# Moving one batch's key sums beside a projection in chunk 1 of a linear attention and GELU feed-forward kernel

## The chip, the cores and the metric

The kernel runs on one core of a Trainium2 chip. The metric is the device time of the whole program in microseconds, the median of several executions. TensorE is called PE below, VectorE DVE, ScalarE ACT, GpSimd POOL and SyncE SP, as in the profile.

## The reference

Linear attention without softmax, an RMS norm per head, and a two-layer feed-forward block with the exact GELU, all in float32:

```python
kv = np.einsum('bhsd,bhse->bhde', k, v)            # 8 batches, 8 heads, 576 tokens, 64 wide
out = np.einsum('bhsd,bhde->bhse', q, kv)
rms = np.sqrt(np.mean(out * out, axis=-1, keepdims=True) + 1e-06)
attn = out / rms * g_norm
x = attn.transpose(0, 2, 1, 3).reshape(4608, 512)
h = x @ w_in                                       # 512 x 2048
g = 0.5 * h * (1 + erf(h / sqrt(2)))
return g @ w_out                                   # 2048 x 512
```

## The kernel before

The 4608 tokens are nine chunks of 512. For each chunk the kernel makes the attention output of the next chunk beside the two layers of this one. The order on every engine is the order in which the code calls the instructions; nothing is reordered, and each engine works through its own queue.

Attention has four steps. `sum_kv` (L176) adds up k^T v of a batch with 80 small matmuls into one PSUM bank, and `place_kv` copies the bank into the SBUF tile `kv[b % 2]`: ACT one copy (L187), DVE two for the swapped halves (L189). `project` (L230) multiplies queries with these, half a chunk's heads at a time, 24 small matmuls into the two banks a0 and a1. `square` and `reduce` give sums of squares (ACT L262, L263, DVE L272), `swap` (ACT L283) and `rsqrt` (DVE, L292 to L314) the norm, and `scale` (DVE L327 and L323) applies it to one of four blocks. For chunks from 2 on, `add_blocks` (L358), `high_block` and `low_block` (L363, L368) then make seven combinations of the blocks, each split into a high and a low half in the fp32r format.

Chunks 0 and 1 do the feed-forward block plainly. A chunk is 16 slots, one per 128 columns of the hidden layer. In slot i, `layer1` does 12 matmuls of 128x512 into one of the two banks h0 and h1 (L662), `gelu` reads it twice (ACT L671, L672), `rest` makes the low half gl of the result (DVE L677), and `second_layer` of the slot before does 12 matmuls (L685), of which every third takes gl. Chunks from 2 on use products of combined 256-wide blocks (seven in place of eight), for which chunk 1 must combine the weights: `sum_weights` adds the blocks of the first layer (DVE L423 and L434; ACT L449 the high half, DVE L455 the low one), as often per slot as `HALVES` says; `sum_out` adds those of the second on POOL (L542), in the slots of `SUMS`; `split_out` splits them (in the kernel before ACT L1018, DVE L1019). SP sends the results to DRAM (L412) and loads what comes next: keys and values in `load_kv` (L130 the main block, 512 KB, L152 the tail, 128 KB), queries (L211), and weights of chunk 2 into a ring (`fetch`, L506) or for good (`keep`, L535).

In chunk 1 (c = 1) the order of a slot is: layer 1 on PE; `spread_matmuls`, which holds projections of chunk 2 and the sums of batch 3; GELU; squares if the slot is in `SQUARES`; `sum_weights` with `rest`; the reduction; `sum_out` and `split_out`; `spread_work` (the norm and the sums of blocks); `second_layer` of the slot before; and `later`, which holds `swap`, the loads and the copies of `place_kv`. Tiles for all these pieces are taken from and given back to one list, `free`, first in, first out, so that a step which takes or gives back earlier changes which tile each later step gets.

Of the kernel before, what the change touches and what calls it, by code (L numbers as in the profile page):

```python
# [37 lines left out]
def linear_attn_rms_gelu_ffn(  # L38
# [19 lines left out]
    B, NP = kv_main.shape[:2]  # L58
# [16 lines left out]
    def bank(name):  # L75
        return psum.tile([P, 512], F32, name=name)

    turn = {"h": 0, "a": 0}

    def next_bank(kind):  # L80

        turn[kind] ^= 1
        return bank(f"{kind}{turn[kind]}")
# [35 lines left out]
    def load_kv(b, p):  # L119

        early = b == 0 or (b == 1 and p > 1)
        if early:
            main = late_tile(f"w_out{NF - 1 - p if b == 0 else NF - 3 - p}")
        elif b == 2 and p > 1:
            main = block_tile(f"s{p - 1}", F32)
        elif b > 2 and p > 1:
            names["keys", p], main = take(stays=True)
        else:
            main = work.tile([P, 2 * DM], I32, name="kv_main", bufs=2).bitcast(F32)
        nc.sync.dma_start(out=main, in_=kv_main[b, p])  # L130
        main = main.rearrange("p (a n) -> p a n", a=2)[:KROWS]
        if b == 0:
            tails = late_tile(f"w_in{NF - 1}")[:TAIL].rearrange("p (a n) -> p a n", a=NP)
            if p == 0:
                nc.sync.dma_start(out=tails, in_=kv_tail[0])
            tail = tails[:, p]
        else:
            at = slice((p - 2) * 2 * P, (p - 1) * 2 * P)
            if early:
                tail = late_tile(f"w_in{NF - 5}")[:, at]  # L140
            elif b == 2 and p > 1:
                if p == 2:
                    kv_ps["tails"] = block_tile("s0", F32)
                tail = kv_ps["tails"][:, at]
            elif b > 2 and p > 1:
                if p == 2:
                    names["keys", 0], kv_ps["tails"] = take(stays=True)
                tail = kv_ps["tails"][:, at]
            else:
                tail = work.tile([P, 2 * P], I32, name="kv_tail", bufs=2).bitcast(F32)  # L150
            tail = tail[:TAIL]
            nc.sync.dma_start(out=tail, in_=kv_tail[b, :, p])  # L152
        tail = tail.rearrange("p (a n) -> p a n", a=2)
        parts = [main[:, :, j * P:(j + 1) * P] for j in range(NJ)] + [tail]
        kv_in[b, p] = [(t[:, 0], t[:, 1]) for t in parts]

    def free_keys():
        free.extend(names.pop(("keys", n)) for n in (2, 3, 0))

    kv_ps = {}  # L160

    def rows(r):
        return slice(r * D, (r + 1) * D)

    def sum_kv(b, pairs, ps=None):

        first = 0
        if ps is None:
            first = pairs[0]
            ps = kv_ps[b, first] = next_bank("a")  # L170
        for p in pairs:
            n = p - first
            for j, (k, v) in enumerate(kv_in.pop((b, p))):

                for r in (slice(0, D), slice(D, 2 * D)):
                    nc.tensor.matmul(  # L176
                        out=ps[r, n * D:(n + 1) * D], lhsT=k[:, r], rhs=v[:, r],
                        start=(j == 0), stop=(j == NJ),
                    )

    def place_kv(b, pairs):

        ps = kv_ps.pop((b, pairs[0]))
        ps = ps[:, :len(pairs) * D].rearrange("p (n d) -> p n d", d=D)
        at = slice(pairs[0], pairs[-1] + 1)
        t = kv[b % 2]
        nc.scalar.copy(out=t[:, at, 0], in_=ps)  # L187
        for r in range(2):
            nc.vector.tensor_copy(out=t[rows(r), at, 1], in_=ps[rows(1 - r)])  # L189
# [196 lines left out]
    def piece(x):  # L386
        return x.rearrange("p (k a n) -> p k a n", k=2, a=2)
# [139 lines left out]
    def take(dtype=F32, stays=False, first=()):  # L527
        name = next(n for n in [*(n for n in first if n in free), *free]
                    if not (stays and n in RINGS))
        free.remove(name)  # L530
        return name, block_tile(name, dtype)[:, :2 * DM]

    def keep(key):
        t = resident[key] = block_tile(KEPT_IN[key[1]], F32R)[:, AWAY:AWAY + 2 * DM]
        nc.sync.dma_start(out=t.bitcast(F32), in_=products[key])  # L535
# [139 lines left out]
    def rest(gh, gl, h):  # L675

        nc.vector.tensor_tensor(out=gl, in0=h, in1=gh.bitcast(F32), op=ALU.subtract)  # L677
        return gh, gl
# [106 lines left out]
    for d in range(0, 2 * D, BLK):  # L785
        h = d // D * D
# [39 lines left out]
    ps = next_bank("a")  # L826
# [47 lines left out]
    for half in range(2):  # L874
# [6 lines left out]
        n = 2 + half  # L881
# [21 lines left out]
    g, h, acc, sums, names = {}, {}, {}, {}, {}  # L903

    def spread_work(c, i):


        nxt = attn[c + 1]
        if c == 0:
            if i in (3, 5, 7, 9):  # L910
                nxt.squares(BLOCKS[i // 2 - 1])
            if i == 11:
                nxt.inv = nxt.rsqrt()
            if 12 <= i < 15:
                for n in ((0,), (1, 2), (3,))[i - 12]:
                    nxt.scale(n)
            if i in (13, 14):
                nxt.split_x(i - 13)
            return
        if i == 7:  # L920
            nxt.inv = nxt.rsqrt()
        for n in {8: (0, 1), 9: (2, 3)}.get(i, ()):
            nxt.scale(n)
        if i == 11:
            names["spots"], t = zip(*(take(stays=True) for _ in range(2)))
            nxt.spots = {"T3": t[0][:, :DM], "T4": t[0][:, DM:], "T2": t[1][:, :DM]}
        for k in {11: ("T3", "T1"), 12: ("T2", "T4")}.get(i, ()):
            nxt.add_blocks(k)
        for n in {13: (0, 4, 5), 14: (1, 2), 15: (3, 6)}.get(i, ()):
            names[c + 1, n], t = take(F32R, True, (f"w_in{i - 1}",))  # L930
            nxt.high_block(n, piece(t))
            nxt.low_block(n, nc.vector)
        if i == 15:
            free.extend(names.pop("spots"))
            LATE.extend(free[-2:])

    def spread_matmuls(c, i):
        nxt = attn[c + 1]
        if i in ((1, 4) if c else (2, 6)):
            nxt.project(i // 4)  # L940
        if i == 10 and not c:
            nxt.swap()
        if i == (8 if c else 12):
            sum_kv(c + 2, range(NP))
            if c:
                free_keys()

    halves = [(j, second) for j in range(NF // 2) for second in range(2)]

# [19 lines left out]
    def raw_out(j):  # L969

        t = [parts["out", 2 * j + n].rearrange("p (a n) -> p a n", a=2) for n in range(2)]
        product_out(place_out(j, 0), t[0][:, :, :HALF])
        product_out(place_out(j, 4), t[1][:, :, :HALF])
        product_out(place_out(j, 3), t[1][:, :, HALF:])
# [51 lines left out]
    def send():  # L1026

        for x in sent:
            if isinstance(x, str):
                free.append(x)  # L1030
            else:
                product_out(*x)
        sent.clear()

    def later(c, i):

        if i in (8, 9):
            raw_out(i - 2)
        if i == 6:
            attn[c + 1].swap()  # L1040
        if i in (3, 4):
            load_kv(c + 2, i - 1)
        if i in (6, 7):
            attn[c + 2].load(i - 6)
        if i == 9:
            place_kv(c + 2, range(NP))
        if i in KEYS_AHEAD:
            load_kv(c + 3, KEYS_AHEAD.index(i))
        send()
        if f"w_in{i}" not in KEPT_OUT:  # L1050
            free.append(f"w_in{i}")
        if i == 4:
            free.append("w_out3")
        for n in {11: (0, 1), 12: (2, 3, 4), 13: (5,)}.get(i, ()):
            fetch(n)
        for n in {10: (0,), 11: (1,), 13: (2,), 15: (3,)}.get(i, ()):
            keep(RESIDENT[n])

    SUMS = {2: 1, 5: 2, 8: 3, 11: 4, 13: 5}
    SPLITS = {2: 0, 3: 1, 6: 2, 9: 3, 12: 4}  # L1060
    SQUARES = (1, 2, 4, 5)
    HALVES = {0: 2, 1: 1, 2: 1, 3: 2, 4: 1, 5: 1, 6: 1, 7: 1, 8: 1, 10: 2, 11: 1, 12: 1, 13: 1, 14: 0}
    KEYS_AHEAD = (9, 10, 12, 14)
    order = list(range(3, len(weights)))

    last = [2]
# [32 lines left out]
    for s in range(PLAIN * NF):  # L1099
        c, i = divmod(s, NF)  # L1100
# [43 lines left out]
        else:  # L1144
            spread_matmuls(c, i)
            g[s] = gelu(h.pop(s))
            nxt, k = attn[c + 1], SQUARES.index(i) if i in SQUARES else None
            if k is not None:
                sq = nxt.square(BLOCKS[k])
            sum_weights(i, HALVES.get(i, 0), lambda: g.update({s: rest(*g[s])}))  # L1150
            if k is not None:
# [180 lines left out]
    for c in range(FAST, NCH):  # L1332
# [4 lines left out]
        for j, second in parts_of_layer1():  # L1337
# [19 lines left out]
            if c == FAST:  # L1357
                if (j, second) in LAST_SPLITS:
                    n = NJ2 - 2 + LAST_SPLITS.index((j, second))
# [7 lines left out]
            if second and j in (1, 3, NJ2 - 1) or (j, second) == (NJ2 - 1, False):  # L1367
                n = j // 2 - (last and not second)
# [69 lines left out]
```

## Time and profile before

| | us |
|---|---|
| Median of three executions | 770.92 (770.61 to 771.04) |
| The profiled execution: its own time | 770.82 |
| Its span from the first to the last instruction | 769.0 |
| PE busy in it | 763.9 |
| DVE busy | 588.2 |
| ACT busy | 368.4 |
| POOL busy | 181.7 |

Chunk 1's slots lie between 113 and 206 us of the span. The chain that ended last goes back from the last instruction, at each step to what released it, and gives each engine its share. In the order of time a row is the start, the time from the start to the last end of the merged instructions, engine, line, operation, output and inputs, shape and count; a bracket gives idle time ahead of it and what ended that.

### The profile page before, as it was taken

To read this page: it belongs to the slowest core of one execution; us is meant where nothing else is said; L and a number is where in the kernel's file an instruction comes from. 1 tells how busy PE (TensorE), PEld (TensorE's weight loads), DVE (VectorE), ACT (ScalarE), POOL (GpSimd) and SP (SyncE) were. 2 spreads that over 40 slices of the span, in tenths; PEclk is the share of its full clock that TensorE was granted. 3 is DMA by queue.
4 is the path that set the end of the run, shared out by engine and by line. 5 is a ranking of instruction groups with operands and counts; after the bars stand their busy time and mean duration, and the time that the engine had idled before them with its cause. 6 is when DMAs were issued, how large, how long until landed. Compare 5 with 4: busy or idle time off the path is not lost.

```text
span 769.0 us, 16770 instructions
## 1 busy us (share of the span) xinstructions
PE 763.9 (99%) x6588; PEld 723.5 (94%) x6588; DVE 588.2 (76%) x1041; ACT 368.4 (48%) x720; POOL 181.7 (24%) x155
## 2 busy tenths in 40 slices
PE   8999999999999999999999999999999999999998
PEld 7888888888899999999999999999999999999998
DVE  3999867989968974889388947795789578965783
ACT  3777635533564543465244714463446343632460
POOL 1000025433737200630045002700270018001200
DMA  9999963869999998999899989988998999799974
GB/s 344 408 407 375 360 199 127 298 233 316 372 332 333 366 397 320 322 325 374 328 331 325 362 342 329 323 289 323 324 336 274 340 321 322 254 315 351 324 245 170
DMA packets 90178, 244.90 MB, mean 318 GB/s; under 512 B 8948, under 2 KB 31988, under 8 KB 90100
## 3 DMA queue, kind: packets, MB, share of 16 engines
q1 hardware_dynamic: 90096, 243.83, 88.5%
q8 instruction: 52, 0.85, 0.4%
q14 instruction: 26, 0.21, 0.1%
q10 hardware_dynamic: 4, 0.00, 0.0%
HBM read 207.09 MB, written 34.08 MB: 314 GB/s over the span
## 4 chain that ended last, share of the span: by engine, by line
PE 98%; DMA 1%; ACT 0%; DVE 0%; issue 0%
PE acc L1221 24%; PE acc L551 22%; PE h L551 13%; PE acc L685 11%; PE a L1221 11%; PE h L662 11%; DMA w_out<-kv_main 1%; PE a L230 1%; PE acc L176 1%; PE a L176 1%; PE h L652 1%; PE acc L230 1%; PE h L820 0%; PE acc L886 0%; PE h L774 0%; ACT gl L809 0%
## 5 line engine op out<-in xcount | busy, mean ns | idle before, releaser
L685 PE MATMUL acc<-w_out,gh 128*128 128x512 f32 x256 | 79.3, 391 | 0.0
L551 PE MATMUL acc<-w_in,w_in 128*128 128x256 f32 x600 | 78.9, 276 | 0.0
L551 PEld LDWEIGHTS acc<-w_in,w_in 128*128 128x128 f32 x600 | 73.0, 188 | 0.1
L662 PE MATMUL h<-x,w_in 128*128 128x512 f32 x264 | 70.3, 390 | 0.0
L662 PEld LDWEIGHTS h<-x,w_in 128*128 128x128 f32 x264 | 49.3, 188 | 10.8 <-issue 0.3
L685 PEld LDWEIGHTS acc<-w_out,gh 128*128 128x128 f32 x256 | 47.7, 188 | 10.2 <-issue 0.2
L685 PE MATMUL acc<-w_out,gl 128*128 128x512 f32 x128 | 49.8, 389 | 0.0
L551 PE MATMUL h<-w_in,w_in 128*128 128x256 f32 x360 | 48.1, 277 | 0.0
L1221 PE MATMUL acc<-w_in,w_in 128*128 128x256 f32 x378 | 47.9, 276 | 0.0
L542 DVE TENSOR_TENSOR gl<-acc,gh 128x256 f32<-128x256 f32 (+1 forms) x77 | 33.9, 441 | 17.4 <-ACT gh L564 13.3
L1221 PEld LDWEIGHTS acc<-w_in,w_in 128*128 128x128 f32 x378 | 45.1, 188 | 0.0
L671 ACT ACTIVATE gh<-h 128x512 fp32r<-128x512 f32 x32 | 19.1, 598 | 53.1 <-PE h L662 53.1
L1221 PE MATMUL acc<-w_in,w_out 128*128 128x256 f32 x354 | 44.4, 276 | 0.0
L551 PEld LDWEIGHTS h<-w_in,w_in 128*128 128x128 f32 x360 | 44.2, 188 | 0.1
L1221 PEld LDWEIGHTS acc<-w_in,w_out 128*128 128x128 f32 x354 | 42.1, 188 | 0.0
L1221 PE MATMUL acc<-w_in,x 128*128 128x256 f32 x324 | 40.8, 276 | 0.0
L1221 PEld LDWEIGHTS acc<-w_in,x 128*128 128x128 f32 x324 | 38.6, 188 | 0.0
L551 PE MATMUL acc<-x,w_in 128*128 128x256 f32 x270 | 37.1, 276 | 0.0
L1188 POOL TENSOR_TENSOR w_in<-x,w_in 128x512 f32<-128x512 f32 x5 | 7.4, 1474 | 113.7 <-ACT x L583 113.7
L551 PEld LDWEIGHTS acc<-x,w_in 128*128 128x128 f32 x270 | 33.6, 188 | 0.0
L262 ACT ACTIVATE sq<-acc 128x512 f32<-128x512 f32 x10 | 6.0, 602 | 57.2 <-PE acc L230 57.2
L272 DVE TRANSPOSE_TENSOR_REDUCE part<-sq 128x16 f32<-128x512 f32 x33 | 23.3, 706 | 12.6 <-ACT sq L262 12.6
(360 smaller groups left out, 1956.2 us busy)
## 6 DMA issues: line engine op xcount, KB each, us to landing
w_in<-products_in SPq DMA_DIRECT2D x168, 512.0 KB, 5.1
w_in<-products_out SPq DMA_DIRECT2D x133, 512.0 KB, 5.3
products_in<-w_in SPq DMA_DIRECT2D x38, 256.0 KB, 5.4
w_in<-w_in SPq DMA_DIRECT2D x16, 512.0 KB, 10.2
w_out<-w_out SPq DMA_DIRECT2D x16, 512.0 KB, 10.2
q<-qT SPq DMA_DIRECT2D x15, 512.0 KB, 6.9
kv_main<-kv_main SPq DMA_DIRECT2D x14, 512.0 KB, 6.4
w_out<-kv_main SPq DMA_DIRECT2D x8, 512.0 KB, 7.0
```

The costliest lines, as they stand in the source:

```text
L176: nc.tensor.matmul(out=ps[r, n * D:(n + 1) * D], lhsT=k[:, r], rhs=v[:, r], start=(j == 0), stop=(j == NJ),)
L230: nc.tensor.matmul(out=ps[rows(h), p % 2 * HALF + a:p % 2 * HALF + e], lhsT=kv[b % 2][rows(half), p, h ^ half], rhs=q[rows(half), h, a:e], ...
L262: nc.scalar.activation(out=sq, in_=ps, func=AF.Square)
L272: nc.vector.tensor_reduce(out=self.part[:, 2 * k[0] + k[1], :], in_=sq.rearrange("p (b d) -> p b d", d=BLK), op=ALU.add, axis=AX.X, apply_ ...
L542: return eng.tensor_tensor(out=out, in0=x, in1=y, op=op)
L551: nc.tensor.matmul(out=out, lhsT=y, rhs=x[:, z, kb], start=first and kb + i == 0, stop=kb == 1 and i == 2, skip_group_check=True,)
L652: nc.tensor.matmul(out=h[:, half * HALF:(half + 1) * HALF], lhsT=ws[i].bitcast(F32)[:, p * P:(p + 1) * P], rhs=at.block((p // 2, half))[:, ...
L662: nc.tensor.matmul(out=h, lhsT=parts["in", i][:, w][:, p * P:(p + 1) * P], rhs=at.x[p][:, x], start=(m + p == 0), stop=(m == 2 and p == NP ...
L671: nc.scalar.activation(out=gh, in_=h, func=AF.Gelu)
L685: nc.tensor.matmul(out=ps, lhsT=x[:, ts], rhs=parts["out", i][:, w], start=(i == 0 and m == 0), stop=(m == 2 and (i == NF - 1 or (i, t) == ...
L1188: eng.tensor_tensor(out=out, in0=x, in1=y, op=op)
L1221: nc.tensor.matmul(out=self.bank[name][a][:, a * HALF:(a + 1) * HALF], lhsT=x[:, at], rhs=y, start=(k in (0, 2, 1) and n + p + m == 0 and ...
```

## The change

In chunk 1 alone: the projection's second half (of chunk 2's attention) goes from slot 4 to slot 6, and batch 3's key sums from slot 8 to slot 6, right behind it. The sums go into the h bank that layer 1 doesn't use at that moment, in place of an a bank, and `place_kv` follows at once, ahead of slot 6's GELU, in place of at the end of slot 9. The squares of the second half go from slots 4 and 5 to 6 and 7, the swap from 6 to 7, the inverse root from 7 to 8, the scaling from slots 8 and 9 to 9 and 10. One weight sum goes from slot 10 to slot 5. Two loads of batch 4's keys come a slot earlier (12 to 11 and 14 to 13), and the tiles of batch 3's keys are given back two slots earlier.

```diff
--- before.py
+++ after.py
@@ -917,9 +917,9 @@
             if i in (13, 14):
                 nxt.split_x(i - 13)
             return
-        if i == 7:
+        if i == 8:
             nxt.inv = nxt.rsqrt()
-        for n in {8: (0, 1), 9: (2, 3)}.get(i, ()):
+        for n in {9: (0, 1), 10: (2, 3)}.get(i, ()):
             nxt.scale(n)
         if i == 11:
             names["spots"], t = zip(*(take(stays=True) for _ in range(2)))
@@ -936,14 +936,17 @@
 
     def spread_matmuls(c, i):
         nxt = attn[c + 1]
-        if i in ((1, 4) if c else (2, 6)):
-            nxt.project(i // 4)
+        if i in ((1, 6) if c else (2, 6)):
+            nxt.project(i // 6 if c else i // 4)
         if i == 10 and not c:
             nxt.swap()
-        if i == (8 if c else 12):
+        if i == 12 and not c:
             sum_kv(c + 2, range(NP))
-            if c:
-                free_keys()
+        if i == 6 and c:
+            ps = kv_ps[c + 2, 0] = bank(f"h{1 - turn['h']}")
+            sum_kv(c + 2, range(NP), ps)
+            free_keys()
+            place_kv(c + 2, range(NP))
 
     halves = [(j, second) for j in range(NF // 2) for second in range(2)]
 
@@ -1036,14 +1039,12 @@
 
         if i in (8, 9):
             raw_out(i - 2)
-        if i == 6:
+        if i == 7:
             attn[c + 1].swap()
         if i in (3, 4):
             load_kv(c + 2, i - 1)
         if i in (6, 7):
             attn[c + 2].load(i - 6)
-        if i == 9:
-            place_kv(c + 2, range(NP))
         if i in KEYS_AHEAD:
             load_kv(c + 3, KEYS_AHEAD.index(i))
         send()
@@ -1058,9 +1059,9 @@
 
     SUMS = {2: 1, 5: 2, 8: 3, 11: 4, 13: 5}
     SPLITS = {2: 0, 3: 1, 6: 2, 9: 3, 12: 4}
-    SQUARES = (1, 2, 4, 5)
-    HALVES = {0: 2, 1: 1, 2: 1, 3: 2, 4: 1, 5: 1, 6: 1, 7: 1, 8: 1, 10: 2, 11: 1, 12: 1, 13: 1, 14: 0}
-    KEYS_AHEAD = (9, 10, 12, 14)
+    SQUARES = (1, 2, 6, 7)
+    HALVES = {0: 2, 1: 1, 2: 1, 3: 2, 4: 1, 5: 2, 6: 1, 7: 1, 8: 1, 10: 1, 11: 1, 12: 1, 13: 1, 14: 0}
+    KEYS_AHEAD = (9, 10, 11, 13)
     order = list(range(3, len(weights)))
 
     last = [2]
```

PE around the projection's second half, in slot 4 before (h, a and acc are PSUM banks, kv the sums of two batches; L230 is the projection):

```order
L662 MATMUL h_1654<-s_1367,w_in_559 128x512
L230 MATMUL a_1667<-q,kv_69 64x128 x2
L230 MATMUL a_1668<-q,kv_68 64x256 x2
L230 MATMUL a_1667<-q,kv_68 64x128 x2
L230 MATMUL a_1667<-q,kv_69 64x128 x2
L230 MATMUL a_1668<-q,kv_68 64x256 x2
L230 MATMUL a_1667<-q,kv_68 64x128 x2
L685 MATMUL acc_1510<-w_out_567,gh 128x512 x2
```

The projection has wide matmuls ahead of it and behind it, and nothing of it is left in slot 4 now. PE around the key sums (L176), in slot 8 before:

```order
L662 MATMUL h_1883<-s_1367,w_in_737 128x512
L176 MATMUL a_1896<-kv_main 64x64 x8
L176 MATMUL a_1896<-kv_tail 64x64 x2
L176 MATMUL a_1896<-kv_main 64x64 x8
L176 MATMUL a_1896<-kv_tail 64x64 x2
L176 MATMUL a_1896<-x_1646 64x64 x8
L176 MATMUL a_1896<-s_1648 64x64 x2
L176 MATMUL a_1896<-x_1715 64x64 x8
L176 MATMUL a_1896<-s_1648 64x64 x2
L685 MATMUL acc_1510<-w_out_774,gh 128x512 x2
```

The sums too have wide matmuls on both sides, write an a bank, and are gone from slot 8 now. PE in slot 6 now, from the last three groups of the projection on:

```order
L230 MATMUL a_1771<-q,kv_69 64x128 x2
L230 MATMUL a_1772<-q,kv_68 64x256 x2
L230 MATMUL a_1771<-q,kv_68 64x128 x2
L176 MATMUL h_1785<-kv_main 64x64 x8
L176 MATMUL h_1785<-kv_tail 64x64 x2
L176 MATMUL h_1785<-kv_main 64x64 x8
L176 MATMUL h_1785<-kv_tail 64x64 x2
L176 MATMUL h_1785<-x_1646 64x64 x8
L176 MATMUL h_1785<-s_1648 64x64 x2
L176 MATMUL h_1785<-x_1697 64x64 x8
L176 MATMUL h_1785<-s_1648 64x64 x2
L685 MATMUL acc_1510<-w_out_679,gh 128x512 x2
```

The projection now goes straight over into the sums, and the sums' output is an h bank; what follows is slot 5's second layer.

DVE from the kv copies of slot 9 to slot 11's gl before (z and w are the staged weight sums, o the attention output, sq a spread norm):

```order
L189 COPY kv1_69<-a0_1896 64x4x64 x2
L434 TENSOR_TENSOR w_2065<-z_1943,z_1945 128x256
L434 TENSOR_TENSOR w_2065<-z_1943,w_1947 128x256
L677 TENSOR_TENSOR gl_2062<-h1_2048,gh_2061 128x512
L423 TENSOR_TENSOR z_2071<-w_in12_928 128x512
L423 TENSOR_TENSOR z_2073<-w_in13_999 128x512
L434 TENSOR_TENSOR w_2075<-z_2073 128x256
L434 TENSOR_TENSOR w_2075<-w_2075,z_2071 128x256
L455 TENSOR_TENSOR w_in2_2069<-w_2065,w_in2_2069 128x2x256
L434 TENSOR_TENSOR w_2118<-z_2071,z_2073 128x256
L434 TENSOR_TENSOR w_2118<-z_2071,w_2075 128x256
L677 TENSOR_TENSOR gl_2113<-h0_2099,gh_2112 128x512
```

The copies open the stretch, and all the rest of it are weight sums and two gl. The same stretch now, from the end of slot 9's work on:

```order
L423 TENSOR_TENSOR z_2067<-w_in12_928 128x512
L423 TENSOR_TENSOR z_2069<-w_in13_999 128x512
L434 TENSOR_TENSOR w_2071<-z_2069 128x256
L434 TENSOR_TENSOR w_2071<-w_2071,z_2067 128x256
L677 TENSOR_TENSOR gl_2064<-h1_2050,gh_2063 128x512
L327 STREAM_TRANSPOSE sq_2075<-y_1964 128x512
L323 TENSOR_TENSOR o_1492<-o_1492,sq_2075 128x512
L327 STREAM_TRANSPOSE sq_2078<-y_1964 128x512
L323 TENSOR_TENSOR o_1492<-o_1492,sq_2078 128x512
L434 TENSOR_TENSOR w_2118<-z_2067,z_2069 128x256
L434 TENSOR_TENSOR w_2118<-z_2067,w_2071 128x256
L677 TENSOR_TENSOR gl_2113<-h0_2099,gh_2112 128x512
```

The two kv copies and one weight sum's low half (L455) with its two adds (L434) have left this stretch, and two scale steps (L327 with L323) stand in it, ahead of slot 11's gl.

ACT from slot 6's GELU on before:

```order
L671 ACTIVATE gh_1781<-h1_1768 128x512
L672 ACTIVATE h1_1768<-h1_1768 128x512
L449 CAST x0_1785<-w_1740 128x2x256
L1018 CAST w_in3_1798<-w_in0_1749 128x2x256
L1018 CAST w_in2_1801<-w_in0_1749 128x2x256
L283 ACTIVATE t_1816<-part_1508 32x64 x4
L671 ACTIVATE gh_1844<-h0_1831 128x512
L672 ACTIVATE h0_1831<-h0_1831 128x512
L449 CAST w_out3_1848<-w_1791 128x2x256
```

No kv copy and no squares stand here; the copy came in slot 9. ACT now, from slot 5's GELU on:

```order
L671 ACTIVATE gh_1713<-h0_1700 128x512
L672 ACTIVATE h0_1700<-h0_1700 128x512
L449 CAST w_in1_1717<-w_1677 128x2x256
L449 CAST x2_1726<-w_1719 128x2x256
L187 COPY kv1_69<-h0_1785 128x4x64
L671 ACTIVATE gh_1829<-h1_1758 128x512
L672 ACTIVATE h1_1758<-h1_1758 128x512
L262 ACTIVATE sq_1833<-a0_1771 128x512
L263 ACTIVATE o_1492<-a0_1771,half_g_71 128x512
L449 CAST w_in3_1836<-w_1732 128x2x256
```

Slot 6's GELU (L671 and L672 of h1_1758) now stands behind the kv copy (L187), which takes the sums of that slot.

## Rows read from the trace of the kernel before

**Rows 1.** The page: busy us, share of the span and instructions of each engine, the DMA packets, and the chain that ended last by engine.

```profile
PE 763.9 (99%) x6588; PEld 723.5 (94%) x6588; DVE 588.2 (76%) x1041; ACT 368.4 (48%) x720; POOL 181.7 (24%) x155
...
DMA packets 90178, 244.90 MB, mean 318 GB/s; under 512 B 8948, under 2 KB 31988, under 8 KB 90100
...
PE 98%; DMA 1%; ACT 0%; DVE 0%; issue 0%
```

**Rows 2.** PE in order of time, slots 3 to 5 of chunk 1 (start us, us, instruction, count): first layer L662, projection L230, second layer L685.

```profile
131.10 0.62 PE L662 MATMUL h<-x,w_in 128*128 128x512 f32 x2
...
136.54 0.62 PE L662 MATMUL h<-x,w_in 128*128 128x512 f32 x2
...
138.81 0.61 PE L662 MATMUL h<-s,w_in 128*128 128x512 f32 x2
139.35 1.09 PE L230 MATMUL a<-q,kv 64*64 64x128 f32 x24
140.38 0.73 PE L685 MATMUL acc<-w_out,gh 128*128 128x512 f32 x2
...
143.23 0.62 PE L662 MATMUL h<-x,w_in 128*128 128x512 f32 x2
```

**Rows 3.** PE in order of time, slot 8 and the start of slot 9: key sums L176.

```profile
159.55 0.62 PE L662 MATMUL h<-x,w_in 128*128 128x512 f32 x2
...
161.81 0.61 PE L662 MATMUL h<-s,w_in 128*128 128x512 f32 x2
162.36 0.69 PE L176 MATMUL a<-kv_main 112*64 112x64 f32 x16
...
164.16 0.64 PE L176 MATMUL a<-x 112*64 112x64 f32 x16
164.62 0.29 PE L176 MATMUL a<-s 128*64 128x64 f32 x4
164.84 0.73 PE L685 MATMUL acc<-w_out,gh 128*128 128x512 f32 x2
...
167.69 0.61 PE L662 MATMUL h<-x,w_in 128*128 128x512 f32 x2
```

**Rows 4.** PE in order of time at the start of chunk 2, where a projection half stands directly ahead of key sums.

```profile
212.37 0.39 PE L685 MATMUL acc<-w_out,gl 128*128 128x512 f32 x1
212.69 1.10 PE L230 MATMUL a<-q,kv 64*64 64x192 f32 x24
213.71 0.69 PE L176 MATMUL acc<-kv_main 112*64 112x64 f32 x16
...
216.20 2.03 PE L551 MATMUL acc<-w_in,w_in 128*128 128x256 f32 x15
```

**Rows 5.** SP's queue in order of time between 145 and 151 us, then the time to landing of the load of line 130 at 147.06 alone, then of that of line 152 at 148.02 alone.

```profile
147.06 0.91 SPq L130 DMA_DIRECT2D x<-kv_main  x1
148.02 1.17 SPq L152 DMA_DIRECT2D s<-kv_tail  x1
...
DMA to landing us min/median/max: 5.7/5.7/5.7
...
DMA to landing us min/median/max: 5.1/5.1/5.1
```

**Rows 6.** A piece of the chain that ended last in order of time (start us, us, what), then PE's order of time there.

```profile
4.77 7.01 DMA w_out<-kv_main
...
11.91 0.69 PE L176 MATMUL a<-w_out 112*64 112x64 f32 x16 [0.18 <-DMA w_out<-kv_main]
```

**Rows 7.** ACT in order of time, slots 9 and 14 (the kv copy; a high half that waits), then DVE's kv copies.

```profile
173.17 0.37 ACT L187 COPY kv<-a 128x256 f32<-128x256 f32 x1
...
197.28 0.62 ACT L363 CAST s<-o 128x512 fp32r<-128x512 f32 x1 [2.77 <-DMA products_in<-s]
...
177.06 0.86 DVE L189 COPY kv<-a 64x256 f32<-64x256 f32 x2
```

**Rows 8.** DVE in order of time, slot 5, then slots 9 to 14.

```profile
148.92 1.60 DVE L455 TENSOR_TENSOR w_in<-w,w_in 128x512 fp32r<-128x512 f32 x1 [0.90 <-DMA products_out<-x]
...
171.73 0.69 DVE L677 TENSOR_TENSOR gl<-h,gh 128x512 fp32r<-128x512 f32 x1 [2.52 <-ACT h L672]
...
174.14 0.70 DVE L327 STREAM_TRANSPOSE sq<-y 128x512 f32<-128x512 f32 x1
...
177.93 0.43 DVE L434 TENSOR_TENSOR w<-z 128x256 f32<-128x256 f32 x1
...
178.61 0.69 DVE L677 TENSOR_TENSOR gl<-h,gh 128x512 fp32r<-128x512 f32 x1
179.21 1.28 DVE L423 TENSOR_TENSOR z<-w_in 128x512 f32<-128x512 f32 x2
...
181.33 0.68 DVE L455 TENSOR_TENSOR w_in<-w,w_in 128x512 fp32r<-128x512 f32 x1
182.05 0.42 DVE L434 TENSOR_TENSOR w<-z 128x256 f32<-128x256 f32 x1
...
190.96 0.68 DVE L677 TENSOR_TENSOR gl<-h,gh 128x512 fp32r<-128x512 f32 x1
...
202.04 0.68 DVE L677 TENSOR_TENSOR gl<-h,gh 128x512 fp32r<-128x512 f32 x1
```

**Rows 9.** Busy time in five stretches that follow each other from 171.7 to 202.0 us: their sum, and DVE's busy time in them.

```profile
sum 30.30, DVE 29.88; mean DVE 5.98
```

**Rows 10.** PE in order of time: the first rows of the second layer of slots 12 and 14.

```profile
192.18 0.61 PE L685 MATMUL acc<-w_out,gh 128*128 128x512 f32 x2
...
203.05 0.62 PE L685 MATMUL acc<-w_out,gh 128*128 128x512 f32 x2
```

**Rows 11.** POOL in order of time: the starts of the second layer's weight sums of slots 5 and 8.

```profile
147.43 2.54 POOL L542 TENSOR_TENSOR x<-w_out 128x512 f32<-128x512 f32 x2 [10.43 <-ACT h L672]
...
163.69 3.00 POOL L542 TENSOR_TENSOR x<-w_out 128x512 f32<-128x512 f32 x2 [9.35 <-ACT h L672]
```

**Rows 12.** SP's queue in order of time: the first two fetches of the ring.

```profile
185.64 1.78 SPq L506 DMA_DIRECT2D w_in<-products_in  x2
```

## The prediction

> **What bounds the kernel now.** I read the page's busy table and chain first, then TensorE's order of time in chunk 1, then what each piece moved there waits for. The table has PE busy 99% of the span and the chain that ended last lies 98% on PE [rows 1]: a saving counts only if it takes work or a gap off PE, and a loss only if it makes PE wait. In chunk 1 a slot is 5.44 us of PE (12 first-layer and 12 second-layer matmuls): from the row at 131.10 to the one at 136.54 [rows 2]. Slot 4, with the projection's second half, lasts 6.69 (136.54 to 143.23) [rows 2]; slot 8, with the key sums, 8.14 (159.55 to 167.69) [rows 3]. So the two blocks cost 1.25 and 2.70, together 3.95 us. PE waits for no other engine at either.
>
> **What the merge saves.** The matmuls themselves stay. What can go is one change from the wide matmuls to the small ones and back. Chunk 2 already has a projection half directly in front of key sums [rows 4]: after the wide matmul at 212.37 the next would be due 0.23 later, at 212.60; the projection starts at 212.69, the sums at 213.71, the next wide ones at 216.20. The pair takes 3.60. Counted the same way, the projection alone takes 1.12 (the pair at 138.81 ends its turn 0.45 later, at 139.26; L685 starts at 140.38 [rows 2]) and the sums alone 2.58 (161.81 + 0.45 = 162.26 to 164.84 [rows 3]): 3.70. Merging saves 0.10, and one of the two slow starts behind a block, 1.25 - 1.12 = 0.13. **Term 1: -0.23 us**; bounds 0 and -0.5 (twice it).
>
> From projection to sums the trace shows no extra gap: 1.02 from the first projection matmul to the first sum [rows 4], and 1.03 from the first projection matmul to the next wide one in slot 4 [rows 2]. The Trainium skill (TensorEngine Tiling (Array Packing), Key Properties) says that a change of tiling mode drains the array, and projection and sums use different tiles; by it the change inside the pair would eat the saving and term 1 would be about 0. I take the row.
>
> **What the sums at slot 6 wait for.** Sums of pair 3 need keys that SP requests in slot 4: the 512 KB block at 147.06, 5.7 us to landing, so 152.76; the tail at 148.02, 5.1 us, so 153.12 [rows 5]. Nothing that SP issues before them is moved, and they follow VectorE's low halves of slot 4, which the change doesn't move either. Where slot 8 needed them at 164.16, the new place needs them earlier: slot 6 begins at 136.54 + 2 x 5.44 = 147.42, the projection 2.81 later as in slot 4 (150.23), the sums 1.02 after that (151.25), pair 3 another 1.80 on (153.05), its tail 2.26 on (153.51) [rows 2 to 4]. A matmul at the kernel's start began at 11.91 for a block that landed at 4.77 + 7.01 = 11.78 [rows 6], 0.13 later. Margins: 0.16 for the block, 0.26 for the tail. **Term 2**: between 0 and +0.45 (a landing later by 0.6, the spread between 5.1 and 5.7, less the margin of 0.16); I take +0.1.
>
> **What stands behind the sums.** They write the h bank that slot 7's layer 1 takes next, so that layer waits for the copies to kv, and ScalarE does its copy before slot 6's GELU. The sums end at 151.25 + 2.48 = 153.73; ScalarE's copy is 0.37 and VectorE's two 0.86 [rows 7]: 155.0. VectorE may come to them late, since slot 5 has a second weight sum now (two 128x512 adds, two 128x256, a low half: 1.28 + 0.68 + 0.68, 2.6 us alone [rows 8] and up to twice that beside POOL [rows 8, 11]); I put that at 154 and the copies' end at 155.3. Meanwhile PE does slot 5's second layer, 2.85 with its slow start (140.38 to 143.23 [rows 2]), so layer 1 is due at 156.6: margin 1.3. GELU of slot 6 moves to 154.4, its low half to 156.6, needed near 160. Cost 0; if this cover went, PE would stop for what VectorE is late beyond 1.3. Squares, swap and inverse root move to slots 6 to 8, where ScalarE and VectorE still catch up every slot. Cost 0.
>
> **What the later scaling costs.** This is the place that I trust least. Scaling of blocks 2 and 3 moves from slot 9 to slot 10, behind the last point where VectorE idles: it waits 2.52 for ScalarE before the gl at 171.73 [rows 8], and over the following 30.30 us it is busy 29.88 [rows 9]. From there on each thing added makes every later gl late. Added between the gl of slot 9 and that of slot 11: two scale steps, 174.14 to 177.06, 2.92. Gone: kv copies (177.06 to 177.93, 0.87), two 128x256 adds (177.93 to 178.61, 0.68), a low half (181.33 to 182.05, 0.72). Net +0.65. Also, POOL's sums of slot 8 start behind that slot's GELU, at 163.69 now [rows 11], which the swap in front of it moves to about 166.2; they then overlap slot 9's work to 173. A 128x512 pass is 0.68 alone and 1.60 beside POOL [rows 8, 11]: 0 to +1.8 for two such passes; I take +0.35. VectorE is then 1.0 later, and 1.2 against PE, which has gained 0.23. Margins: slot 12's gl ends at 190.96 + 0.68 = 191.64 and is the third matmul from 192.18, so due at 192.63, 0.99 spare; slot 14's ends at 202.72, due 203.05 + 0.45 = 203.50, 0.78 spare [rows 8, 10]. Waits on PE don't add up, since each gives VectorE time: the largest overrun counts, 1.2 - 0.78 = 0.4, less the 0.1 that term 2 gives VectorE already. **Term 3: +0.3**; bounds 0 (lateness under 0.55) and 0.65 + 1.8 + 0.23 - 0.78 = +1.9.
>
> **What moves on SP.** Loads for batch 4 go ahead of the first three fetches in slot 11 and of two in slot 13. They are 640 KB each, some 2 us of transfer at the page's mean of 318 GB/s [rows 1]; the first fetch goes out at 185.64 [rows 12], over 17 us ahead of the last second layer of chunk 1 but one (203.05 [rows 10]), so 0. The stores behind them may land 2 us later; a cast that waits for such a store now ends its wait at 197.28 [rows 7], ahead of slot 14's GELU, whose result PE wants at 203.05: still 0, over 3 us to spare.
>
> **Sum**: -0.23 + 0.1 + 0.3 = +0.2 on the profiled execution's 770.82, which stands 0.10 under the median of 770.92: 771.0. A measurement of this kernel tells about 0.2%, 1.5 us, from no change.
>
> **Rivals.**
> 1. *VectorE's late gl, slower than before.* Place: the second layer of slots 12 to 14. It decides from a lateness of 0.78 - 0.23 = 0.55 against now; every microsecond beyond is one on PE. At the bound, +1.9 - 0.23 + 0.1: 772.6, just over 0.2%. For it: no idle time after 171.73 [rows 9]. Against: POOL's overlap only moves, and what runs beside it in slot 9 leaves slot 8. Chance 0.12, 0.05 of it over 0.2%.
> The Trainium skill (SBUF — State Buffer, Who interferes with whom) calls the port that VectorE and GpSimd share an exclusive lock on which the later one stops fully. By it a pass would pay a whole POOL pass of 1.3 on top, an estimate of 2.0 where the row has 1.60, and this rival would end near 773.
> 2. *Late keys.* PE stands in front of pair 3's sums. If SP's request came one store later (0.5 to 1.5 us), +0.4 to +1.3: 771.3 to 772.2. For it: margins of 0.16 and 0.26. Against: nothing ahead of the request moves. Chance 0.10, 0.02 over 0.2%.
> 3. *The freed tiles go round in another order* from slot 5 to the end, and a cast meets a store that hasn't landed: one such wait was 2.77 on ScalarE [rows 7], without touching PE. With 1 to 2 of it on PE: 772 to 773. Chance 0.04, 0.02 over 0.2%.
> 4. *The merge doesn't save a switch*, the change between projection and sums costing as much: 771.2. Chance 0.05.
> 5. *It is worth over 0.2%.* The two blocks cost 3.95 us with all their matmuls, which stay, so I see no place for it: 769.3 or less, 0.02.
>
> **How the numbers follow.** The forecast, 770.5 to 771.8, has 0.67. The range runs from term 1 alone, less the runs' scatter of 0.3, to most of rival 1: 770.3 to 772.4. Slower by over 0.2%: 0.05 + 0.02 + 0.02 = 0.09. Faster: 0.02. Within 0.2%: 0.89.
>
> **What would show it.** Slot 4 at 5.44 and slot 6 near 9.2 (5.44 + 3.73) prove term 1. A wait of PE for a load of kv_main in slot 6 shows term 2. Waits of PE's second layer for VectorE's L677 in slots 12 to 14 show term 3. Wrong would be: PE without any such wait and a time over 771.8, a wait in front of slot 7's layer 1, or any gap in chunks 2 to 8.

## The result and the profile after

The changed kernel takes **777.85 us** (median of 6 runs, 775.48 to 778.41) against 770.71 (770.48 to 771.04) for the kernel before in the same session: ratio 1.0089, interval 1.0078 to 1.0099, so 7.1 us slower and outside the predicted range. The profiled execution has a span of 776.1 us where before had 769.0. The page's chain that ended last, answering to [rows 1]:

```profile
PE 91%; DVE 4%; DMA 4%; issue 1%; ACT 1%; SPq 0%; DVEq 0%; ACTq 0%
```

The chain now leaves PE for 9% of the span, where before it did for 2%. The table of what PE waited for (us in total, times, longest) names the new places:

```profile
PE h L551 <- DVE gl L677: 3.5, 1, 3.5
...
PE acc L685 <- DVE gl L677: 0.8, 2, 0.6
```

**The merged block.** PE in order of time, slot 4 and slots 6 to 7 of chunk 1, answering to [rows 2, 3]:

```profile
136.32 0.62 PE L662 MATMUL h<-x,w_in 128*128 128x512 f32 x2
...
141.76 0.61 PE L662 MATMUL h<-x,w_in 128*128 128x512 f32 x2
...
147.22 0.61 PE L662 MATMUL h<-x,w_in 128*128 128x512 f32 x2
...
153.14 0.69 PE L176 MATMUL h<-x 112*64 112x64 f32 x16
...
156.77 0.62 PE L662 MATMUL h<-x,w_in 128*128 128x512 f32 x2
```

Slot 4 is 5.44 us, as announced. Slot 6 is 9.55 (147.22 to 156.77); 9.17 were due. The chain that ended last, in two stretches, says what was late (start us, us, what):

```profile
146.75 6.35 DMA x<-kv_main
...
200.53 1.24 DVE x L455
...
202.15 7.31 DMA products_in<-x
...
209.56 0.62 ACT x L363
...
211.20 0.70 DVE gl L677
```

The first row is pair 3's keys: they landed at 153.10 and PE used them at 153.14. The others are the loss itself, at the end of chunk 1: VectorE's low half of slot 13's weight sum (L455, into tile x1), its store, a ScalarE cast, slot 15's GELU and low half, and only then the first layer of chunk 2. ScalarE in order of time, answering to the cast of [rows 7]:

```profile
200.44 0.62 ACT L363 CAST w_in<-o 128x512 fp32r<-128x512 f32 x1 [4.99 <-DMA products_in<-w_in]
...
209.56 0.62 ACT L363 CAST x<-w_in 128x512 fp32r<-128x512 f32 x1 [4.76 <-DMA products_in<-x]
210.09 0.59 ACT L671 ACTIVATE gh<-h 128x512 fp32r<-128x512 f32 x1
```

Before there was one long wait of this kind, 2.77 us [rows 7]; now there are two of 4.99 and 4.76, and the second stands ahead of slot 15's GELU. The cast writes slot 14's operand piece into x1, the tile that slot 13's sums had just given back while their store was still under way. PE's first layer of chunk 2 (L551) started 1.02 us after the projection (L230) before:

```profile
205.87 1.10 PE L230 MATMUL a<-q,kv 64*64 64x192 f32 x24
206.89 3.10 PE L551 MATMUL h<-w_in,w_in 128*128 128x256 f32 x24
209.83 0.63 PE L685 MATMUL acc<-w_out,gh 128*128 128x512 f32 x2
```

Now it starts 4.56 us after it (207.38 to 211.94).

**The clock.** The two windows behind that stop (us, busy us of each engine, granted clock, DMA share, GB/s), and PE in order of time:

```profile
213.00:215.00 2.00, 2.00 (x13) 2.00 (x12) 2.00 (x3) 0.67 (x2) 1.92 (x2) 0.53 0.41 107
215.00:217.00 2.00, 2.00 (x10) 1.92 (x10) 1.19 (x4) 1.18 (x2) 1.92 (x4) 0.61 0.89 328
```

```profile
211.94 1.97 PE L551 MATMUL h<-w_in,w_in 128*128 128x256 f32 x12 [3.46 <-DVE gl L677]
...
216.27 0.76 PE L685 MATMUL acc<-w_out,gh 128*128 128x512 f32 x2
```

The 24 matmuls of the first layer took 4.33 us (211.94 to 216.27); before they took 2.94 (206.89 to 209.83). TensorE had idled 3.46 us, and soon after it took up work again the granted clock fell to about its lower level, 1.2 GHz.

**VectorE.** The inverse root on VectorE, first before (its first and its last operation), then now, and POOL beside it now:

```profile
159.46 0.22 DVE L292 SCALAR_TENSOR_TENSOR m<-part,t 128x64 f32<-128x64 f32 x1
...
161.51 0.22 DVE L305 SCALAR_TENSOR_TENSOR y<-t,y 128x64 f32<-128x64 f32 x1
```

```profile
168.13 1.31 DVE L292 SCALAR_TENSOR_TENSOR m<-part,t 128x64 f32<-128x64 f32 x1
169.47 0.75 DVE L299 TENSOR_SCALAR y<-m 128x64 int32<-128x64 int32 x1
170.25 0.82 DVE L305 SCALAR_TENSOR_TENSOR t<-y 128x64 f32<-128x64 f32 x1
...
173.28 0.23 DVE L305 SCALAR_TENSOR_TENSOR y<-t,y 128x64 f32<-128x64 f32 x1
```

```profile
166.36 3.00 POOL L542 TENSOR_TENSOR w_in<-w_out 128x512 f32<-128x512 f32 x2 [11.86 <-ACT h L672]
169.44 0.73 POOL L542 TENSOR_TENSOR w_in<-w_in 128x256 f32<-128x256 f32 x1
170.25 0.74 POOL L542 TENSOR_TENSOR w_in<-w_in,w_in 128x256 f32<-128x256 f32 x1
```

The nine operations take 5.38 us (168.13 to 173.51) in place of 2.27 (159.46 to 161.73 before). The low halves that follow are late, and PE's second layer stops for them (PE in order of time, answering to [rows 10]):

```profile
187.49 0.50 PE L685 MATMUL acc<-w_out,gl 128*128 128x512 f32 x1 [0.15 <-DVE gl L677]
...
199.45 0.50 PE L685 MATMUL acc<-w_out,gl 128*128 128x512 f32 x1 [0.61 <-DVE gl L677]
```

**The account** goes by PE's starts, from slot 13 of chunk 0, ahead of all that the change moves, to the first layer of chunk 2: 109.81 us before (97.08 to 206.89), 115.08 after (96.86 to 211.94), so +5.27.

| where | us |
|---|---|
| the merge: the two blocks' 3.95 against the 3.75 that an undisturbed merged block adds (a_rsqrt_keys) | -0.20 |
| slot 5 | +0.02 |
| slot 6, 9.55 against 9.19 | +0.36 |
| slot 11 | +0.03 |
| slots 12 to 14, which hold the second layers of slots 11 to 13: their excess over 5.44 | +1.53 |
| the stop ahead of chunk 2, 4.56 against 1.02 | +3.54 |

Behind it come +1.39 by the clock in the 24 matmuls and +0.13 in the rows right behind them, and +0.47 in chunk 3. The last is a stretch in which TensorE was slower; two other profiles have one like it at other places, so it is not counted as the change's (last section).

### The profile page after: what moved, and what is told of

Its sections match the earlier page's. It is cut to its first block, busy times and chain, and to the rows that moved or that the text cites. A ratio compares the mean times of both kernels' runs of the same rounds, so it can differ in the third digit from the quotient of the medians.

```text
span 776.1 us, 16783 instructions
## 1 busy us (share of the span) xinstructions
PE 766.2 (99%) x6588; PEld 724.9 (93%) x6588; DVE 590.2 (76%) x1041; ACT 368.4 (47%) x720; POOL 179.7 (23%) x155
## 4 chain that ended last, share of the span: by engine, by line
PE 91%; DVE 4%; DMA 4%; issue 1%; ACT 1%; SPq 0%; DVEq 0%; ACTq 0%
PE acc L1222 24%; PE acc L551 22%; PE h L551 13%; PE a L1222 11%; PE acc L685 8%; PE h L662 7%; DMA w_out<-kv_main 1%; PE acc L176 1%; PE a L230 1%; DMA products_in<-x 1%; PE h L652 1%; PE acc L230 1%; DMA x<-kv_main 1%; PE a L176 1%; DVE w L434 1%
## 5 line engine op out<-in xcount | busy, mean ns | idle before, releaser
L685 PE MATMUL acc<-w_out,gh 128*128 128x512 f32 x256 | 79.5, 392 | 0.0
L662 PE MATMUL h<-x,w_in 128*128 128x512 f32 x264 | 70.3, 391 | 0.0
L1222 PE MATMUL acc<-w_in,w_in 128*128 128x256 f32 x486 | 61.3, 277 | 0.0
L662 PEld LDWEIGHTS h<-x,w_in 128*128 128x128 f32 x264 | 49.4, 188 | 10.7 <-ACT w_in L638 0.3
L551 PE MATMUL acc<-w_in,w_in 128*128 128x256 f32 x420 | 58.4, 277 | 0.0
L1222 PEld LDWEIGHTS acc<-w_in,w_in 128*128 128x128 f32 x486 | 57.9, 188 | 0.0
L685 PEld LDWEIGHTS acc<-w_out,gh 128*128 128x128 f32 x256 | 48.0, 189 | 9.9 <-issue 0.2
L551 PEld LDWEIGHTS acc<-w_in,w_in 128*128 128x128 f32 x420 | 52.5, 188 | 0.1
L685 PE MATMUL acc<-w_out,gl 128*128 128x512 f32 x128 | 50.3, 393 | 0.8 <-DVE gl L677 0.8
L551 PE MATMUL acc<-x,w_in 128*128 128x256 f32 x330 | 46.4, 276 | 0.0
L551 PE MATMUL acc<-w_out,w_in 128*128 128x256 f32 x300 | 42.2, 277 | 0.0
L671 ACT ACTIVATE gh<-h 128x512 fp32r<-128x512 f32 x32 | 19.1, 598 | 47.6 <-PE h L662 47.6
L551 PEld LDWEIGHTS acc<-x,w_in 128*128 128x128 f32 x330 | 41.5, 188 | 0.0
L551 PE MATMUL h<-w_in,w_in 128*128 128x256 f32 x252 | 36.2, 283 | 3.5 <-DVE gl L677 3.5
L551 PEld LDWEIGHTS acc<-w_out,w_in 128*128 128x128 f32 x300 | 37.7, 188 | 0.0
L1222 PE MATMUL acc<-w_in,w_out 128*128 128x256 f32 x294 | 37.3, 277 | 0.0
L551 PEld LDWEIGHTS h<-w_in,w_in 128*128 128x128 f32 x252 | 32.4, 192 | 3.7 <-DVE gl L677 3.6
L1222 PEld LDWEIGHTS acc<-w_in,w_out 128*128 128x128 f32 x294 | 35.2, 188 | 0.0
```

The costliest lines, as they stand in the source:

```text
L551: nc.tensor.matmul(out=out, lhsT=y, rhs=x[:, z, kb], start=first and kb + i == 0, stop=kb == 1 and i == 2, skip_group_check=True,)
L662: nc.tensor.matmul(out=h, lhsT=parts["in", i][:, w][:, p * P:(p + 1) * P], rhs=at.x[p][:, x], start=(m + p == 0), stop=(m == 2 and p == NP ...
L671: nc.scalar.activation(out=gh, in_=h, func=AF.Gelu)
L685: nc.tensor.matmul(out=ps, lhsT=x[:, ts], rhs=parts["out", i][:, w], start=(i == 0 and m == 0), stop=(m == 2 and (i == NF - 1 or (i, t) == ...
L1222: nc.tensor.matmul(out=self.bank[name][a][:, a * HALF:(a + 1) * HALF], lhsT=x[:, at], rhs=y, start=(k in (0, 2, 1) and n + p + m == 0 and ...
```

## The experiments

Theory A: the stop is a matter of which tile the free list hands to a ScalarE cast. Theory B: VectorE is late, and whichever tile it is, TensorE pays.

| run | median us | before, same session | ratio, 95% interval |
|---|---|---|---|
| a_s0_piece | 772.74 | 770.62 | 1.0028 [1.0018, 1.0037] |
| a_keys_back | 772.48 | 770.62 | 1.0023 [1.0014, 1.0032] |
| b_keys_early | 775.56 | 770.62 | 1.0060 [1.0047, 1.0073] |
| a_filler | 775.55 | 770.62 | 1.0065 [1.0052, 1.0077] |
| a_rsqrt | 772.01 | 770.86 | 1.0016 [1.0007, 1.0024] |
| a_rsqrt_keys | 771.52 | 770.86 | 1.0010 [1.0002, 1.0019] |
| a_apart | 773.87 | 770.86 | 1.0035 [1.0021, 1.0048] |
| a_norm | 771.52 | 771.07 | 0.9998 [0.9989, 1.0008] |
| b_keys_tile | 770.75 | 771.07 | 0.9997 [0.9985, 1.0010] |

The ratio follows the means of the executions, so it is not always the ratio of the two medians.

### a_s0_piece: another tile for one cast

```diff
-            names[c + 1, n], t = take(F32R, True, (f"w_in{i - 1}",))
+            names[c + 1, n], t = take(F32R, True, (f"w_in{i - 1}", *(("s0",) if i == 14 else ())))
```

> The changed kernel, with one tile picked by hand: slot 14's second operand piece takes s0 (the scratch tile of POOL's sums, no store in flight) where the free list gives x1 (low sums of slot 13, stores in flight until 209.5); slot 15's second piece then takes x1. Theory A (a ScalarE cast stands in front of slot 15's GELU until a store out of its tile has landed, and TensorE stops for it): the cast no longer waits, TensorE's 3.46 us in front of chunk 2 go, and with them the 1.39 us at the low granted clock: 777.85 - 4.85 = 773.0. Theory B (VectorE is late by the moved scaling and every late piece of work costs TensorE, whichever tile): 776 to 778, with another wait in the place of this one.

772.74: 5.1 us of the 7.1 are gone, as A said. ScalarE in order of time:

```profile
204.23 0.62 ACT L363 CAST s<-w_in 128x512 fp32r<-128x512 f32 x1
205.40 0.60 ACT L671 ACTIVATE gh<-h 128x512 fp32r<-128x512 f32 x1 [0.56 <-PE h L662]
...
209.27 0.62 ACT L363 CAST x<-w_out 128x512 fp32r<-128x512 f32 x1 [2.25 <-DMA products_in<-x]
```

The GELU now waits for PE and not for a store. x1 still had to wait for its store, but as slot 15's piece, with no GELU behind it, and the granted clock of the run is 1.0.

### a_keys_back and b_keys_early: the key loads' slots, undone and alone

```diff
-    KEYS_AHEAD = (9, 10, 11, 13)
+    KEYS_AHEAD = (9, 10, 12, 14)
```

> The changed kernel with the loads of batch 4's keys put back to slots 9, 10, 12 and 14. The free list then gives slot 14's second piece w_in8, out of which slot 12's split stored (a slot older). Theory A: as with the picked tile, 773.0 (772.5 to 773.5); slot 13's cast still waits for slot 12's low sums, which costs TensorE nothing by itself. Theory B: 776 to 778.

772.48: as A said, at the low end of its span. The reverse edit in the kernel before:

> The kernel before with nothing but the loads of batch 4's keys moved to slots 9, 10, 11 and 13. The free list then gives slot 14's second piece w_in9, the tile of slot 13's low sums, whose stores go out at about 199.5 to 200.4. Theory A: landing 5 to 7 us later, 204.5 to 207.7, then the GELU and the low half of slot 15, 2.1 us: TensorE, due at 206.89, waits 0 to 2.9 us and may lose up to 1.4 us to the clock: 771 to 775, most likely 773. Theory B: VectorE has nothing more to do than before: 770.7.

775.56, just above the span of 771 to 775 that was given, with VectorE's work unchanged. Its chain (start us, us, what), then PE in order of time and a window:

```profile
199.64 8.01 DMA products_in<-w_in
...
207.75 0.62 ACT w_in L363
```

```profile
210.12 4.61 PE L551 MATMUL h<-w_in,w_in 128*128 128x256 f32 x24 [3.35 <-DVE gl L677]
...
214.57 0.63 PE L685 MATMUL acc<-w_out,gh 128*128 128x512 f32 x2
```

```profile
211.00:213.00 2.00, 2.00 (x12) 2.00 (x11) 2.00 (x3) 0.84 (x2) 1.92 (x2) 0.50 0.15 56
```

Two numbers in a table of slots bring back the stop (3.35 us) and the slow matmuls behind it (4.45 us, 210.12 to 214.57, at a clock of 0.50, the lower level). B falls: nothing of VectorE's was moved here. The estimate of 773 was short because the store landed at 207.65, at the late end of the 204.5 to 207.7 assumed, and the clock took its full price (4.45 against 2.93 in the undisturbed kernels: 1.52).

### b_keys_tile: the loads early, the tile changed

In b_keys_early, slot 14's second piece asks for w_in6 first.

> As b_keys_early (the kernel before with the earlier key loads alone, 775.56), with slot 14's second piece in w_in6 (POOL's scratch tile, no store in flight) in place of w_in9. Theory A (the tile, and not the loads' new place in SP's queue): 770.8. If the loads' place counts (the ring's fetches or the stores landing later): 772 to 775.5.

770.75, the kernel before's own time. In its profile the way from slot 13 of chunk 0 to the first layer of chunk 2 takes 109.82 us (97.02 to 206.84), against 109.81 before. (The profiled execution itself took 773.58; what it lost lies between 655 and 730 us, see the last section.) So neither the loads' place in SP's queue nor the fetches behind them cost anything that can be measured; the tile is the whole of it.

### a_filler: work for TensorE in the gap

```diff
             attn[c + 1].project(0, [bank(f"a{half}") for half in range(2)])
+            idle, w = bank("h1"), parts["out", NF - 1]
+            for _ in range(14):
+                nc.tensor.matmul(out=idle, lhsT=w[:, :P], rhs=w[:, :DM], start=True, stop=True, ...)
```

> The changed kernel with 14 wide matmuls (128x512, 0.227 us each, 3.2 us) whose results nobody reads, into the idle bank of the first layer, in the gap in which TensorE waits in front of chunk 2. If the granted clock of 0.53 to 0.61 in 213 to 217 comes from that gap: the next 24 matmuls take 2.94 us in place of 4.33, 776.5. If it has another reason: 777.9. If the filler delays the next matmuls: up to 778.4.

775.55, 2.3 us under the changed kernel. PE in order of time:

```profile
209.27 3.47 PE L1271 MATMUL h<-w_out 128*128 128x512 f32 x14
212.71 1.68 PE L551 MATMUL h<-w_in,w_in 128*128 128x256 f32 x12
...
215.64 0.63 PE L685 MATMUL acc<-w_out,gh 128*128 128x512 f32 x2
```

The 24 matmuls take 2.93 us (212.71 to 215.64), with a granted clock of 1.00 in every window there: the idle time was what lowered it. With the rows right behind, that accounts for 1.5 of the 2.3. The two profiles differ in two more places, neither of them the filler's doing: slot 6 took 9.19 and not 9.55, as the keys came in time, and the slower stretch of chunk 3 (0.47) is missing. The profiled execution took 776.59, the most of the five; its slot 13 of chunk 0 starts 1.22 us later than in the changed kernel (98.08 against 96.86), behind a granted clock of 0.66 from 10 to 15 us, which the changed kernel's profile doesn't have. The changed kernel's own runs point the same way: the one of six that had a mean clock of 1.0 took 775.48, those at 0.996 to 0.998 took 777.75 to 778.41.

### a_rsqrt and a_norm: what made VectorE late

> The changed kernel with the loads of batch 4's keys put back (772.48 as measured), and the inverse root issued on VectorE at the head of slot 8, ahead of that slot's low half, where VectorE idles 1.83 us and POOL's sums have not yet begun. Theory C (term 3 is the inverse root: its nine small operations took 5.4 us beside POOL's sums in the place of 2.2 alone, and nothing later makes that up): VectorE is 1.5 to 3 us earlier in slots 10 to 13, the three stops of TensorE in slots 11 to 13 (0.48 + 0.14 + 0.91 = 1.53 us longer slots) go: 771.0 (770.7 to 771.3). Rival D (term 3 is the moved scaling and whatever POOL then overlaps): 772.2 to 772.6, the stops stay.

772.01: 0.5 us less than a_keys_back, a third of the 1.5 that C said. The stops of the second layers of slots 11 to 13 (they stand in slots 12 to 14) are gone, but the head of slot 8 brought a new one: slot 8's own low half now stands behind the root, and PE stops 0.68 us for it at 171.66, which makes slot 8 0.97 us longer (6.41). D falls: the scaling stayed in slots 9 and 10, where D had the stops stay too. VectorE, then POOL, in a_rsqrt_keys, which has the same order:

```profile
166.09 0.23 DVE L305 SCALAR_TENSOR_TENSOR y<-t,y 128x64 f32<-128x64 f32 x1
166.34 1.27 DVE L305 SCALAR_TENSOR_TENSOR t<-y 128x64 f32<-128x64 f32 x1
167.65 1.22 DVE L314 TENSOR_TENSOR t<-t,m 128x64 f32<-128x64 f32 x1
168.90 0.78 DVE L305 SCALAR_TENSOR_TENSOR y<-t,y 128x64 f32<-128x64 f32 x1
```

```profile
166.24 2.54 POOL L542 TENSOR_TENSOR w_in<-w_out 128x512 f32<-128x512 f32 x2 [9.76 <-ACT h L672]
168.86 0.73 POOL L542 TENSOR_TENSOR w_in<-w_in 128x256 f32<-128x256 f32 x1
```

Six operations fit in front of POOL at 0.19 to 0.23 us; from 166.24 on, each lasts as long as one of POOL's passes (1.27 beside passes of 2.54 / 2). The root began at 164.82 and would have needed until 167.09 alone: the mechanism holds, the remedy came 0.85 us late. In a_norm, the squares of blocks 2 and 3 are both taken in slot 6, swap and root in slot 7, scaling in slots 8 and 9.

> As a_rsqrt_keys, but the squares of blocks 2 and 3 are both taken in slot 6, the swap and the inverse root in slot 7 behind its low half, the scaling in slots 8 and 9 as in the kernel before. The root's nine operations then run in the stretch of slot 7 in which POOL is idle: 2.2 us in place of 5.0. Theory (the merge saves 0.2 us, and all the rest was the cost of what it moved): no stop of TensorE for VectorE in slots 6 to 15, the way from slot 1 of chunk 1 to the first fast matmul of chunk 2 takes 109.6 us where the kernel before takes 109.81; the time 0.2 us under before, not to be told from it by the runs. If the root was not the cause: a stop stays somewhere in slots 8 to 13 and the time is 771.2 to 772.5.

The root ran from 164.00 to 166.28, 2.28 us. PE's list of waits names no low half of chunk 1 any more, and PE in order of time reads:

```profile
97.22 0.96 PE L662 MATMUL h<-x,w_in 128*128 128x512 f32 x3
...
206.85 1.33 PE L551 MATMUL h<-w_in,w_in 128*128 128x256 f32 x9
```

109.63 us, against 109.81 before: -0.18, as forecast (both from slot 13 of chunk 0, which the forecast calls slot 1 of chunk 1). The ratio of the times, 0.9998 [0.9989, 1.0008], can't show a gain of that size and doesn't.

### a_rsqrt_keys and a_apart: terms 2 and 1 by themselves

Both have the root at the head of slot 8 and the later key loads put back, as in a_rsqrt. New in a_rsqrt_keys:

```diff
-        if i in (3, 4):
-            load_kv(c + 2, i - 1)
+        if i == 3:
+            load_kv(c + 2, 2)
+            load_kv(c + 2, 3, ("x2",))
```

> The same, and pair 3's keys of batch 3 are loaded in slot 3 behind pair 2's (into tile x2) in place of slot 4. If term 2 is TensorE's wait for that load: slot 6 falls from 9.87 us to 9.17 (5.44 + 1.25 + 2.70 - 0.23), and the time by 0.4 to 0.7: 770.4 (770.0 to 770.8), the kernel before within 0.2%. If something else lengthens slot 6: as a_rsqrt.

> The same as a_rsqrt_keys with the merge alone undone: the projection's second half back in slot 4, the key sums stay in slot 6. If the merge saves 0.23 us: slot 4 takes 6.69 and slot 6 8.14, together 14.83 against 5.44 + 9.17 = 14.61; the time 0.2 us above a_rsqrt_keys, which the runs can hardly tell and the two profiles can. If it saves nothing: the two slots sum to 14.61 here too.

PE in order of time, first a_rsqrt_keys (slot 6), then a_apart (slots 4 and 6):

```profile
147.46 0.62 PE L662 MATMUL h<-x,w_in 128*128 128x512 f32 x2
...
156.65 0.62 PE L662 MATMUL h<-x,w_in 128*128 128x512 f32 x2
```

```profile
136.56 0.62 PE L662 MATMUL h<-x,w_in 128*128 128x512 f32 x2
...
143.24 0.61 PE L662 MATMUL h<-x,w_in 128*128 128x512 f32 x2
...
148.68 0.61 PE L662 MATMUL h<-x,w_in 128*128 128x512 f32 x2
...
156.83 0.39 PE L662 MATMUL h<-x,w_in 128*128 128x512 f32 x1
```

With the keys loaded in slot 3, slot 6 takes 9.19 and not 9.87 as in a_keys_back: term 2 is the wait for keys. Its size differs from one execution to the next: with the load left in slot 4, slot 6 took 9.19 in a_filler, 9.47 in a_rsqrt and 9.75 in a_s0_piece. The 771.52 missed the 770.4 by about the stop at slot 8's low half, which stayed. Unmerged, the two slots take 6.68 + 8.15 = 14.83; merged 5.44 + 9.19 = 14.63: term 1 is -0.20. The median of a_apart doesn't show it, since its stop at slot 8's low half grew to 2.1 us (the root slid further under POOL), and its six executions scatter from 771.82 to 774.75.

## Why the prediction was wrong

- **The step that failed** is "What moves on SP": that a cast which waits for a store ends its wait "over 3 us to spare" ahead of need. It took the one wait of [rows 7] and pushed it 2 us. But the edit of KEYS_AHEAD changes which tile each cast gets: the free list is first in, first out, and two tiles taken a slot earlier hand slot 14's piece the tile that slot 13 has just stored from. Here the wait, 4.76 us to 209.56, stands ahead of slot 15's GELU, the last of the chunk, and the first layer of chunk 2 waits for that slot's low half. Rival 3 named this mechanism with 0.04 and 1 to 2 us; it was 3.54 us on PE, and 1.39 by the clock. Picking the tile (a_s0_piece, b_keys_tile) and moving the loads (a_keys_back, b_keys_early) show it from both sides. The prediction had named its sign, a gap in chunks 2 to 8. Without this step the kernel takes 772.48 (a_keys_back), still just above the range's 772.4, by terms 2 and 3.
- **The clock** was in no term. A stop of some 3.4 us brought another 1.5 us behind it in both kernels that had it (1.39 + 0.13 here, 1.52 in b_keys_early).
- **Term 3** (+0.3, bounds 0 and +1.9) had the mechanism and missed its size: 1.56. It priced the moved scaling and two wide passes beside POOL, and gave "squares, swap and inverse root" a cost of 0. The root's nine operations, 2.27 us alone, took 5.38 beside POOL's sums of slot 8. It also looked at the low halves of slots 12 and 14; the largest stop was slot 13's, and the stops did add up (0.44 + 0.18 + 0.91).
The Trainium skill (SBUF — State Buffer, Who interferes with whom) calls the port pair that VectorE shares with GpSimd an exclusive lock. The root's rows agree: operations that take 0.20 and 0.23 us alone took 0.75 beside a POOL pass of 0.73 and 0.82 beside one of 0.74. The prediction applied the rule to the wide passes alone.
- **Term 2** (+0.1, bounds 0 and +0.45): right in kind, 0.36 in this trace; the load took 6.35 us to land in place of 5.7. In a_keys_back the tail came late too, and slot 6 took 0.68 more than in a_rsqrt_keys.
- **Term 1** (-0.23) measured -0.20, by a_apart against a_rsqrt_keys, and -0.18 over the whole of chunk 1, by a_norm against the kernel before.
The Trainium skill (TensorEngine Tiling (Array Packing), Key Properties) says that a change of tiling mode drains the array. A drain between projection and sums that ate the saving, as the prediction's rival 4 had it, shows in neither trace, and the measurement decides.
- **What stands behind the sums** cost nothing, as said: VectorE's kv copies ended at 155.26, 1.5 us ahead of slot 7's first layer at 156.77.

## What to carry to other kernels

In a kernel whose tiles come from a shared free list, a load that is moved by a slot moves every later tile choice: list which tile each later writer gets, and which store last left it, before you call the move free. Look hardest at the last slot of a stage, where a wait has no later slot to be absorbed in. And price short vector operations by what runs beside them, not by their own length.

## What the runs showed of the hardware

- After idling 3.4 to 3.5 us TensorE worked at a granted clock of 0.50 to 0.61 in the windows shown (changed kernel and b_keys_early), busy throughout; with the gap filled it stayed at 1.00.
- An operation of 0.2 us on VectorE took 0.66 to 1.31 us beside POOL, about the length of one POOL pass.
- Stores issued behind three ring fetches took 7.31 and 8.01 us to land in the two chains shown.
- Three profiles have a stretch in which 12 matmuls of 128x256 took 1.41 us where they take 1.36 elsewhere, at a granted clock of 1.00: the changed kernel's from 366 to 378 us (+0.47), a_rsqrt's from 282 to 292 (with the short gap ahead of it, +0.64) and b_keys_tile's from 655 to 730 (+2.83). It stands at another place each time, and its cause stays open.
